# First pass of a feed-forward stage: two result tiles of a block opened side by side, in PSUM banks of their own behind the attention

## The chip, the cores and the metric

One core of a Trainium2 chip runs the whole program. The metric is device time in microseconds (us), from the start of an execution to its end; the median of several executions counts. The engines are TensorE (PE; its weight loads, PEld, overlap its matmuls), VectorE (DVE), ScalarE (ACT), GpSimd (POOL) and SyncE (SP), which here only issues DMAs.

## The reference

Three stages in a row, all in fp32, on 4 x 576 = 2304 tokens of width 512 (8 heads of 64):

```python
scores = where(causal, -1e9, q @ k.T / 8);  a = softmax(scores)
local = a @ v
mem = (phi(q) @ M_prev) / (phi(q) . z_prev + 1e-6)          # phi = elu + 1
x = sigmoid(beta) * mem + (1 - sigmoid(beta)) * local        # to [2304, 512]

x = relu(x @ w_in) ** 2 @ w_out                              # w_in [512, 2048], w_out [2048, 512]

order = argsort(-(x @ w_gate))                               # [2304, 8], greedy, 288 tokens for each expert
out[mask_e] = relu(x[mask_e] @ w1[e]) @ w2[e]                # 8 experts, w1 [512, 1024], w2 [1024, 512]
```

## The kernel before, in words

Matmuls keep fp32 accuracy by splitting each operand into a high and a low half of a narrower float type (`split`, line 23: ACT copies the high half, DVE or POOL subtracts it to get the low one) and multiplying three times (`mm3`, lines 41 to 45: high x high, high x low, low x high).

**Attention** (`attention`, line 48) goes over 16 pairs of heads, in steps that work on several pairs at once. Between its own matmuls it calls `fill` (line 1065), which lets the feed-forward stage put matmuls of its own into TensorE's order. Its PSUM pool has six of the eight banks.

**The feed-forward stage** (class `Ffn`, line 389) runs over 16 chunks of 128 hidden columns in three passes (`PASSES`, line 369: chunks 0 to 5, 6 to 9, 10 to 15), since the split weights of all chunks don't fit beside the rest. The weights come as 64-bit floats, which `weights` (line 411) loads and `narrow` (line 29) converts, with steps on ACT and DVE, a temporary tile `r`, and a last step on POOL.

*The first pass* (`first`, line 464) takes the tokens in eight blocks of 288. `tokens` (line 430) loads a block's attention result (`xf`), adds its halves on POOL, splits it (`xs`, one buffer), and stores it to `xs_d` for the later passes. `hidden` (line 442) multiplies one chunk: 12 matmuls into a PSUM tile `ph` (pool `ffp3`, two banks), then ACT's relu (`r`, line 450), POOL's square (`gf`, line 452) and the split into `gs` on ACT and DVE (lines 25 and 26). After the six chunks come four result tiles, d = 0 to 3, of 128 result columns each (`output`, line 457): 6 chunks x 3 matmuls = 18 matmuls into a tile of the same two banks, ACT's eviction into `yo` (line 483; two buffers, for even and odd d), and SP's store to `yp_d` (line 484). The call of `tokens` for the next block stands ahead of d = 1, or of a later d when the attention has not yet gone far enough. A block is thus 72 hidden and 72 output matmuls.

About four and a half blocks go through `fill` while the attention runs; the rest follows behind it, in a loop (lines 1092 to 1098) that puts in a piece of the conversion of the next pass' weights after every 48 matmuls (temporary tiles `r` in a PSUM pool `cvp` of three banks, raw tiles in `cv`, two buffers).

*The later passes* (`later`, line 486) take the tokens in six steps of 384 per pass. `get` (line 492) loads a step's tokens from `xs_d` into `xt` (line 495; two buffers, 1.5 MB each): the load for step n + 1 is traced after the first hidden tile of step n. Each step loads the sums so far (`y`, line 505), adds its four result tiles to them on DVE (line 522), and stores them again.

**The third stage** (class `Moe`) finds the tokens of each expert (routing) and runs the experts; it starts with the gate's logits, which are taken from the last pass' sums.

**What sets the order of the work.** TensorE's order is that of the program text up to the end of the first pass (`manual_schedule`, line 1081); behind it, and on all other engines and on SP, a scheduler fixes each engine's order when the program is built. On the chip every engine goes through its order and stands at each instruction until what it needs is there. Memory of closed pools is used again; a new tile there waits for the last use of those tiles that lay in the same place (`reuse_waits="tile"`). Before, the two `xt` buffers lie in memory that the attention left; the pool `ga` of `gs` tiles for the later passes and the pool of `y` tiles lie in memory that the first pass leaves.

Of the kernel before, what the change touches and what calls it, by code (L numbers as in the profile page):

```python
# [7 lines left out]
F32 = mybir.dt.float32  # L8
F32R = mybir.dt.float32r
I32 = mybir.dt.int32  # L10
BF16 = mybir.dt.bfloat16
AF = mybir.ActivationFunctionType
OP = mybir.AluOpType
PSUM = bass.MemoryType.PSUM
# [8 lines left out]
def split(nc, hi, lo, src, eng=None):  # L23

    nc.scalar.activation(hi, src, AF.Copy)  # L25
    (eng or nc.vector).tensor_tensor(lo, src, hi.bitcast(F32), op=OP.subtract)  # L26
# [14 lines left out]
def mm3(nc, out, lhi, llo, rhi, rlo, start, stop):  # L41

    nc.tensor.matmul(out, lhi, rhi, start=start, stop=False)  # L43
    nc.tensor.matmul(out, lhi, rlo, start=False, stop=False)  # L44
    nc.tensor.matmul(out, llo, rhi, start=False, stop=stop)  # L45
# [316 lines left out]
TB = 288  # L362
NB_T = NT // TB
TW = 384
NB_W = NT // TW
FF = 2048
KD = DM // 128
KF = FF // 128
PASSES = tuple(tuple(range(a, b)) for a, b in ((0, 6), (6, 10), (10, KF)))
GB = 7  # L370
# [9 lines left out]
def run(work):  # L380

    while True:
        try:
            next(work)
        except StopIteration as e:
            return e.value


class Ffn:
# [5 lines left out]
    def __init__(self, tc, ctx, ident, x_d, xs_d, w_in, w_out, w_gate, yp_d, y_d, lg):  # L395
        self.tc, self.nc, self.ident = tc, tc.nc, ident
        self.x_d, self.xs_d, self.w_in, self.w_out, self.yp_d, self.y_d, self.lg = x_d, xs_d, w_in, w_out, yp_d, y_d, lg
        nc = tc.nc
        one = self.one = ctx.enter_context(tc.tile_pool(name="ff1", bufs=1, side="right"))
        self.two = ctx.enter_context(tc.tile_pool(name="ff2", bufs=2, side="right"))  # L400
        self.p3 = ctx.enter_context(tc.tile_pool(name="ffp3", bufs=2, space=PSUM, side="right"))
        self.start = None
        wg = one.tile([128, KD, 8], F32, name="wg")
        nc.sync.dma_start(wg, w_gate.rearrange("(k p) e -> p k e", p=128))
        self.wgs = one.tile([128, KD, 16], F32R, name="wgs")
        split(nc, self.wgs[:, :, 0:8], self.wgs[:, :, 8:16], wg)
        self.two8 = one.tile([16, 8], F32, name="two8")
        nc.vector.tensor_tensor(self.two8, ident[0:16, 0:8], ident[0:16, 8:16], op=OP.add)
        self.win, self.wout, self.Y, self.have = {}, {}, {}, 0
# [44 lines left out]
        split(nc, G[:, 0], G[:, 1], gf)  # L454
        return G

    def output(self, py, G, cs, d):
        nc, ds = self.nc, slice(128 * d, 128 * d + 128)
        for c in cs:
            w = self.wout[c]  # L460
            mm3(nc, py, w[:, 0, ds], w[:, 1, ds], G[c][:, 0], G[c][:, 1], c == cs[0], c == cs[-1])
            yield 3

    def first(self, gpool):

        nc, xs, cs = self.nc, {}, PASSES[0]
        for i in range(NB_T):
            while self.have <= i:
                yield 0
            if i not in xs:  # L470
                xs[i] = self.tokens(i)
                for _ in range(LAG):
                    yield 0
            G = {}
            for c in cs:
                G[c] = yield from self.hidden(xs[i], c, gpool)
            for d in range(KD):
                if d >= 1 and i + 1 < NB_T and i + 1 not in xs and self.have > i + 1:
                    xs[i + 1] = self.tokens(i + 1)
                py = self.p3.tile([128, TW], F32, name="ph")[:, 0:TB]  # L480
                yield from self.output(py, G, cs, d)
                yo = self.start.tile([128, TB], F32, name=f"yo{d % 2}")
                nc.scalar.activation(yo, py, AF.Copy)
                nc.sync.dma_start(self.yp_d[128 * d:128 * d + 128, TB * i:TB * i + TB], yo)

    def later(self, gpool, beside):


        nc, steps = self.nc, [(p, i) for p in range(1, len(PASSES)) for i in range(NB_W)]
        xs, G, after = {}, {}, []  # L490

        def get(n):
            if n < len(steps):
                t_ = xs[n] = self.xp.tile([128, 2, KD, TW], F32R, name="xt")
                nc.sync.dma_start(t_.bitcast(F32), self.xs_d[:, :, :, TW * steps[n][1]:TW * steps[n][1] + TW])
                G[n] = {}

        def hide(n, c):
            G[n][c] = run(self.hidden(xs[n], c, gpool))

        get(0)
        for n, (p, i) in enumerate(steps):
            cs, final = PASSES[p], p == len(PASSES) - 1
            y = self.Y[i] = self.ty.tile([128, KD, TW], F32, name="y")
            nc.sync.dma_start(y, self.yp_d[:, TW * i:TW * i + TW].rearrange("(k p) t -> p k t", p=128))
            for c in cs:
                if c not in G[n]:
                    hide(n, c)
                if c == cs[0]:
                    get(n + 1)  # L510
                if c == cs[1]:
                    for w in after:
                        w()
                    after = []
                if c % 2 == 0:
                    next(beside, None)
            if n + 1 < len(steps):
                hide(n + 1, PASSES[steps[n + 1][0]][0])
            for d in range(KD):
                py = self.p2x.tile([128, TW], F32, name="py")  # L520
                run(self.output(py, G[n], cs, d))
                nc.vector.tensor_tensor(y[:, d], py, y[:, d], op=OP.add)  # L522
            if not final:
                nc.sync.dma_start(self.yp_d[:, TW * i:TW * i + TW].rearrange("(k p) t -> p k t", p=128), self.Y.pop(i))
            else:
                after = [lambda i=i: self.logits(i)]
                if i < NB_W - HELD:
                    after.append(lambda i=i: run(self.rows(i)))
            del G[n], xs[n]
        for w in after:  # L530
            w()
# [504 lines left out]
def tile_attention_ffn_moe(ctx, tc, q, k, v, M_prev, z_prev, beta, w_in, w_out, w_gate, w1, w2, out):  # L1036
    nc = tc.nc
# [13 lines left out]
    fctx = ExitStack()  # L1051
    f = Ffn(tc, fctx, ident, x_d, xs_d, w_in, w_out, w_gate, yp_d, y_d, lg)
    wa = fctx.enter_context(tc.tile_pool(name="wa", bufs=6, side="right"))

    def chunks(cs, home, pool, psum=None):
        for c in cs:
            for part in range(2):
                yield from f.weights(c, part, home, pool, nc.gpsimd, psum)
# [22 lines left out]
    with tc.manual_schedule(engines=INORDER):  # L1081
        attention(tc, ident, q, k, v, M_prev, z_prev, beta, x_d, fill, ended)
        m.open(ctx, lg)
        f.have = NB_T
        wb = fctx.enter_context(tc.tile_pool(name="wb", bufs=4, reuse_waits="tile"))
        cv = fctx.enter_context(tc.tile_pool(name="cv", bufs=2, reuse_waits="tile"))
        f.t2 = fctx.enter_context(tc.tile_pool(name="ff22", bufs=2, reuse_waits="tile"))
        f.xp = fctx.enter_context(tc.tile_pool(name="ffx", bufs=2, reuse_waits="tile"))
        pctx = ExitStack()
        cp = pctx.enter_context(tc.tile_pool(name="cvp", bufs=3, space=PSUM, side="right", reuse_waits="tile"))  # L1090
        conv, done = chunks(PASSES[1], wb, cv, cp), 0
        for e in work:
            done += e
            if done >= PIECE:
                done -= PIECE
                next(conv, None)
        for _ in conv:
            pass
        pctx.close()
    sctx.close()  # L1100
    f.p2x = fctx.enter_context(tc.tile_pool(name="ffp2x", bufs=2, space=PSUM, side="right", reuse_waits="tile"))
    ga = fctx.enter_context(tc.tile_pool(name="ga", bufs=GB, side="right", reuse_waits="tile"))
    f.ty = fctx.enter_context(tc.tile_pool(name="ffy", bufs=HELD + 1, side="right", reuse_waits="tile"))
    f.later(ga, chunks(PASSES[2], wa, cv))
    held = (x for i in range(NB_W - HELD, NB_W) for x in f.rows(i))

# [37 lines left out]
```

## Time and profile before

| | us |
|---|---|
| median of 3 runs | 1079.33 (1076.73 to 1083.37) |
| the profiled execution | 1079.72 |
| its span, from the first to the last instruction | 1077.60 |

The profile is one execution. Times in it are us from the span's start unless marked ns. A row of the timeline names start, duration, engine, line, operation, the tile written and the tiles read, with shapes (partitions x elements); a bracket behind it gives the idle time of the engine just before it and what ended that. Matmuls are pipelined: the next one starts before the last one's end, and the marked idle time counts from that end.

### The profile page before, as it was taken

The numbers are of one execution on the slowest core, as the hardware profiler recorded it, in microseconds if no ns is written. First come the engines' busy times: TensorE is split into PE (matmuls) and PEld (weight loads), VectorE is DVE, ScalarE is ACT, GpSimd is POOL, SyncE is SP. The second block draws the span as 40 slices with busy tenths as digits, with TensorE's granted clock in tenths as the row PEclk, the third lists the DMA queues.
The fourth block names the chain that finished last, engine by engine and source line by source line (L and its number), as shares of the span: only waits on it lengthen the run. The fifth ranks groups of instructions, "written<-read, shape, count | busy, mean of one in ns | idle before, by whom it ended". The sixth has DMA issues, their size and how long they took to land.

```text
span 1077.6 us, 19670 instructions
## 1 busy us (share of the span) xinstructions
PE 966.5 (90%) x7025; PEld 890.5 (83%) x7025; DVE 641.1 (59%) x1876; ACT 553.0 (51%) x1363; POOL 520.2 (48%) x498
## 2 busy tenths in 40 slices
PE   4766799999999988999999999997399999989996
PEld 3555588887898987999999999995298888889996
DVE  7998888788888846565222222235775677655110
ACT  6776888887888744453222333321243443344531
POOL 3665665656556535354122121110565865677841
PEclk9667899999999999999999999996589999999998
DMA  5453465364635287676463332101542455437411
GB/s 147 120 145 104 110 155 156 85 181 93 173 77 145 61 293 243 189 241 240 171 216 117 117 117 74 75 1 59 179 157 68 156 179 179 135 111 235 152 30 30
DMA packets 147393, 148.62 MB, mean 138 GB/s; under 512 B 69472, under 2 KB 119648, under 8 KB 147296
## 3 DMA queue, kind: packets, MB, share of 16 engines
q1 hardware_dynamic: 144224, 137.93, 41.6%
q0 software_dynamic: 3072, 9.44, 2.8%
q8 instruction: 55, 0.90, 0.3%
q14 instruction: 42, 0.34, 0.1%
HBM read 109.60 MB, written 37.75 MB: 137 GB/s over the span
## 4 chain that ended last, share of the span: by engine, by line
PE 56%; DVE 18%; issue 8%; DMA 7%; ACT 6%; POOL 3%; SPq 1%; another core or an unknown queue 0%; POOLq 0%; ACTq 0%; DVEq 0%
PE ph L945 11%; PE ph L43 6%; PE ph L44 6%; PE ph L45 6%; PE py L44 4%; PE py L43 4%; PE py L45 4%; PE ps L311 3%; DMA wraw<-in_moe_w_dram 3%; PE ps L216 2%; POOL wsp L928 2%; PE rs L727 2%; DVE P L227 2%; DVE ptb L26 2%; DVE qpt L199 2%
## 5 line engine op out<-in xcount | busy, mean ns | idle before, releaser
L452 POOL TENSOR_TENSOR gf<-r 128x384 f32<-128x384 f32 (+1 forms) x108 | 87.3, 810 | 228.8 <-ACT r L450 222.5
L928 POOL TENSOR_TENSOR wsp<-wraw,wsp 128x1024 fp32r<-128x1024 f32 x64 | 150.8, 2386 | 47.2 <-ACT wsp L926 47.0
L945 PE MATMUL ph<-xs,wsp 128*128 128x288 f32 x768 | 122.0, 309 | 0.0
L26 DVE TENSOR_TENSOR gs<-gf,gs 128x384 fp32r<-128x384 f32 (+1 forms) x108 | 60.7, 564 | 97.9 <-ACT gs L25 97.7
L945 PE MATMUL ph<-hs,wsp 128*128 128x288 f32 x768 | 115.9, 304 | 0.7 <-ACT hs L968 0.6
L945 PEld LDWEIGHTS ph<-xs,wsp 128*128 128x128 f32 x768 | 108.4, 195 | 5.3 <-issue 4.2
L245 POOL TENSOR_SCALAR P<-P,R,og 128x128 f32<-128x128 f32 (+2 forms) x144 | 95.4, 677 | 33.5 <-DVE R L243 13.6
L945 PEld LDWEIGHTS ph<-hs,wsp 128*128 128x128 f32 x768 | 105.4, 191 | 2.6 <-issue 0.9
L926 ACT ACTIVATE wsp<-wraw 128x1024 fp32r<-128x1024 f32 x64 | 64.2, 1051 | 57.3 <-DMA wraw<-in_moe_w_dram 38.9
L450 ACT ACTIVATE r<-ph 128x384 f32<-128x384 f32 (+1 forms) x108 | 48.3, 450 | 83.5 <-PE ph L45 82.0
L239 ACT ACTIVATE P<-P,R 128x128 f32<-128x128 f32 (+2 forms) x144 | 83.2, 579 | 10.9 <-DVE R L227 9.2
L25 ACT ACTIVATE gs<-gf 128x384 fp32r<-128x384 f32 (+1 forms) x108 | 52.6, 487 | 62.7 <-POOL gf L452 50.7
L44 PE MATMUL py<-gs,wout 128*128 128x384 f32 x240 | 81.0, 338 | 0.1
L44 PE MATMUL ph<-xt,win 128*128 128x384 f32 x240 | 80.8, 337 | 0.0
L45 PE MATMUL ph<-xt,win 128*128 128x384 f32 x240 | 80.8, 337 | 0.0
L43 PE MATMUL ph<-xt,win 128*128 128x384 f32 x240 | 80.7, 336 | 0.0
L45 PE MATMUL py<-gs,wout 128*128 128x384 f32 x240 | 80.5, 336 | 0.0
L43 PE MATMUL py<-gs,wout 128*128 128x384 f32 x240 | 79.2, 338 | 0.3 <-DVE y L522 0.3
L270 PE MATMUL ps<-ident,P 128*128 128x128 f32 x320 | 62.7, 305 | 12.5 <-POOL P L245 4.8
L216 PE MATMUL ps<-kt,qt 64*128 64x128 f32 (+3 forms) x384 | 59.4, 390 | 14.7 <-DVE ptb L26 7.0
L43 PE MATMUL ph<-xs,win 128*128 128x288 f32 x192 | 62.2, 324 | 4.0 <-ACT r L450 1.9
L26 DVE TENSOR_TENSOR ptb<-ps,ptb 128x384 fp32r<-128x384 f32 (+3 forms) x128 | 59.5, 467 | 8.9 <-ACT ptb L25 7.2
(227 smaller groups left out, 2537.2 us busy)
## 6 DMA issues: line engine op xcount, KB each, us to landing
wraw<-in_moe_w_dram SPq DMA_DIRECT2D x32, 1024.0 KB, 9.6
xt<-xs_d SPq DMA_DIRECT2D x12, 1536.0 KB, 7.7
x_d<-xo SPq DMA_DIRECT2D x32, 288.0 KB, 3.5
xf<-x_d SPq DMA_DIRECT2D x32, 288.0 KB, 3.5
xs_d<-xs SPq DMA_DIRECT2D x8, 1152.0 KB, 6.7
y<-yp_d SPq DMA_DIRECT2D x12, 768.0 KB, 6.4
raw<-in_moe_w_in_dram SPq DMA_DIRECT2D x16, 512.0 KB, 3.8
raw<-in_moe_w_out_dram SPq DMA_DIRECT2D x16, 512.0 KB, 3.6
```

The lines of the kernel that those rows point to most:

```text
L26: (eng or nc.vector).tensor_tensor(lo, src, hi.bitcast(F32), op=OP.subtract)
L43: nc.tensor.matmul(out, lhi, rhi, start=start, stop=False)
L44: nc.tensor.matmul(out, lhi, rlo, start=False, stop=False)
L45: nc.tensor.matmul(out, llo, rhi, start=False, stop=stop)
L216: nc.tensor.matmul(ps[j][:, 0:w], qt[r0, a, qs], kt[r0, b, 0:w], start=i == 0, stop=i == 2)
L239: nc.scalar.activation(pw, pw, AF.Exp, bias=R[:, 0, u:u + 1], scale=-1.0, accum_out=R[:, 1, u:u + 1])
L245: nc.gpsimd.tensor_scalar(PP[n][w], PP[n][w], R[:, 2, w:w + 1], og9[:, hp, w:w + 1], op0=OP.mult, op1=OP.mult)
L270: nc.tensor.transpose(tr[:, 128 * i:128 * i + 128], P[:, 128 * i:128 * i + 128], ident)
L452: nc.gpsimd.tensor_tensor(gf, r, r, op=OP.mult)
L926: nc.scalar.activation(w[:, 0, hs], raw[:, hs], AF.Copy)
L928: eng.tensor_tensor(w[:, 1, hs], raw[:, hs], w[:, 0, hs].bitcast(F32), op=OP.subtract)
L945: nc.tensor.matmul(out, l[a], r[b], start=i + p == 0, stop=i == n - 1 and p == 2)
```

## The change

In `first`, the result tiles are taken in three groups: d = 0 and 1 together, then 2, then 3. The tiles of a group are opened together; each takes the first four chunks in turn, then each takes the last two and is evicted. `tokens` for the next block is called ahead of d = 2 or 3. As long as the attention runs, the result tiles come from the two `ph` banks as before; behind it they come from a pool `ffpo` with two banks of its own, and `cvp` has two banks instead of three.

The two `xt` buffers become two pools of one buffer: the first in memory that the attention left, the second in memory that the first pass leaves. `ga` changes to memory that the attention left; the pool `ff22` (tiles of `logits` and `rows`) changes to memory that the first pass leaves.

```diff
--- before.py
+++ after.py
@@ -399,7 +399,7 @@
         one = self.one = ctx.enter_context(tc.tile_pool(name="ff1", bufs=1, side="right"))
         self.two = ctx.enter_context(tc.tile_pool(name="ff2", bufs=2, side="right"))
         self.p3 = ctx.enter_context(tc.tile_pool(name="ffp3", bufs=2, space=PSUM, side="right"))
-        self.start = None
+        self.start, self.pout, self.po = None, self.p3, "ph"
         wg = one.tile([128, KD, 8], F32, name="wg")
         nc.sync.dma_start(wg, w_gate.rearrange("(k p) e -> p k e", p=128))
         self.wgs = one.tile([128, KD, 16], F32R, name="wgs")
@@ -454,9 +454,9 @@
         split(nc, G[:, 0], G[:, 1], gf)
         return G
 
-    def output(self, py, G, cs, d):
+    def output(self, py, G, cs, d, part=slice(None)):
         nc, ds = self.nc, slice(128 * d, 128 * d + 128)
-        for c in cs:
+        for c in cs[part]:
             w = self.wout[c]
             mm3(nc, py, w[:, 0, ds], w[:, 1, ds], G[c][:, 0], G[c][:, 1], c == cs[0], c == cs[-1])
             yield 3
@@ -474,14 +474,17 @@
             G = {}
             for c in cs:
                 G[c] = yield from self.hidden(xs[i], c, gpool)
-            for d in range(KD):
-                if d >= 1 and i + 1 < NB_T and i + 1 not in xs and self.have > i + 1:
+            for ds in ((0, 1), (2,), (3,)):
+                if ds[0] and i + 1 < NB_T and i + 1 not in xs and self.have > i + 1:
                     xs[i + 1] = self.tokens(i + 1)
-                py = self.p3.tile([128, TW], F32, name="ph")[:, 0:TB]
-                yield from self.output(py, G, cs, d)
-                yo = self.start.tile([128, TB], F32, name=f"yo{d % 2}")
-                nc.scalar.activation(yo, py, AF.Copy)
-                nc.sync.dma_start(self.yp_d[128 * d:128 * d + 128, TB * i:TB * i + TB], yo)
+                py = {d: self.pout.tile([128, TW], F32, name=self.po)[:, 0:TB] for d in ds}
+                for part in (slice(0, 4), slice(4, None)):
+                    for d in ds:
+                        yield from self.output(py[d], G, cs, d, part)
+                        if part.stop is None:
+                            yo = self.start.tile([128, TB], F32, name=f"yo{d % 2}")
+                            nc.scalar.activation(yo, py[d], AF.Copy)
+                            nc.sync.dma_start(self.yp_d[128 * d:128 * d + 128, TB * i:TB * i + TB], yo)
 
     def later(self, gpool, beside):
 
@@ -491,7 +494,7 @@
 
         def get(n):
             if n < len(steps):
-                t_ = xs[n] = self.xp.tile([128, 2, KD, TW], F32R, name="xt")
+                t_ = xs[n] = self.xp[n % 2].tile([128, 2, KD, TW], F32R, name="xt")
                 nc.sync.dma_start(t_.bitcast(F32), self.xs_d[:, :, :, TW * steps[n][1]:TW * steps[n][1] + TW])
                 G[n] = {}
 
@@ -1084,10 +1087,12 @@
         f.have = NB_T
         wb = fctx.enter_context(tc.tile_pool(name="wb", bufs=4, reuse_waits="tile"))
         cv = fctx.enter_context(tc.tile_pool(name="cv", bufs=2, reuse_waits="tile"))
-        f.t2 = fctx.enter_context(tc.tile_pool(name="ff22", bufs=2, reuse_waits="tile"))
-        f.xp = fctx.enter_context(tc.tile_pool(name="ffx", bufs=2, reuse_waits="tile"))
+        x0 = fctx.enter_context(tc.tile_pool(name="ffx0", bufs=1, reuse_waits="tile"))
+        ga = fctx.enter_context(tc.tile_pool(name="ga", bufs=GB, reuse_waits="tile"))
         pctx = ExitStack()
-        cp = pctx.enter_context(tc.tile_pool(name="cvp", bufs=3, space=PSUM, side="right", reuse_waits="tile"))
+        cp = pctx.enter_context(tc.tile_pool(name="cvp", bufs=2, space=PSUM, side="right", reuse_waits="tile"))
+        f.pout = pctx.enter_context(tc.tile_pool(name="ffpo", bufs=2, space=PSUM, side="right", reuse_waits="tile"))
+        f.po = "po"
         conv, done = chunks(PASSES[1], wb, cv, cp), 0
         for e in work:
             done += e
@@ -1099,8 +1104,10 @@
         pctx.close()
     sctx.close()
     f.p2x = fctx.enter_context(tc.tile_pool(name="ffp2x", bufs=2, space=PSUM, side="right", reuse_waits="tile"))
-    ga = fctx.enter_context(tc.tile_pool(name="ga", bufs=GB, side="right", reuse_waits="tile"))
     f.ty = fctx.enter_context(tc.tile_pool(name="ffy", bufs=HELD + 1, side="right", reuse_waits="tile"))
+    x1 = fctx.enter_context(tc.tile_pool(name="ffx1", bufs=1, side="right", reuse_waits="tile"))
+    f.t2 = fctx.enter_context(tc.tile_pool(name="ff22", bufs=2, side="right", reuse_waits="tile"))
+    f.xp = x0, x1
     f.later(ga, chunks(PASSES[2], wa, cv))
     held = (x for i in range(NB_W - HELD, NB_W) for x in f.rows(i))
```

## Rows read from the trace of the kernel before

**Rows 1.** The page, section 1: busy us, share of the span, instructions.
```profile
PE 966.5 (90%) x7025; PEld 890.5 (83%) x7025; DVE 641.1 (59%) x1876; ACT 553.0 (51%) x1363; POOL 520.2 (48%) x498
```

**Rows 2.** Stretches: length, busy PE, PEld, DVE, ACT, POOL; PE clock, DMA, GB/s.
```profile
383.00:462.00 79.00, 69.77 (x475) 66.00 (x475) 40.24 (x62) 37.04 (x85) 34.26 (x37) 0.96 0.74 239
462.00:718.00 256.00, 255.88 (x1486) 250.05 (x1485) 87.61 (x158) 85.80 (x169) 62.89 (x69) 1.00 0.42 143
```

**Rows 3.** The same view, shorter stretches behind the attention.
```profile
392.10:400.60 8.50, 8.35 (x60) 8.12 (x61) 5.39 (x9) 5.13 (x14) 4.51 (x6) 1.00 0.97 325
...
424.50:431.00 6.50, 3.58 (x20) 2.66 (x19) 6.50 (x11) 2.96 (x7) 3.85 (x5) 0.89 0.49 156
431.00:436.30 5.30, 5.30 (x24) 5.30 (x24) 3.87 (x7) 3.31 (x7) 3.61 (x4) 0.50 0.74 220
```

**Rows 4.** TensorE's waits from 383 to 462: us in total, times, longest.
```profile
PE ph L44 <- DVE gs L26: 3.7, 6, 1.4
PE ph L43 <- ACT r L450: 1.9, 2, 1.7
PE ph L43 <- ACT yo L483: 1.8, 1, 1.8
PE ph L43 <- ACT gs L25: 1.4, 3, 0.5
```

**Rows 5.** TensorE's timeline: starts of result tiles, and chunk 5's low half in one.
```profile
400.62 0.29 PE L43 MATMUL ph<-gs,wout 128*128 128x288 f32 x1
...
424.54 0.30 PE L43 MATMUL ph<-gs,wout 128*128 128x288 f32 x1
...
430.56 0.61 PE L44 MATMUL ph<-gs,wout 128*128 128x288 f32 x1 [0.89 <-DVE gs L26]
430.96 0.44 PE L45 MATMUL ph<-gs,wout 128*128 128x288 f32 x1
431.20 0.44 PE L43 MATMUL ph<-gs,wout 128*128 128x288 f32 x1
...
450.63 0.30 PE L43 MATMUL ph<-gs,wout 128*128 128x288 f32 x1
...
457.36 0.30 PE L43 MATMUL ph<-gs,wout 128*128 128x288 f32 x1
...
459.75 0.29 PE L43 MATMUL ph<-gs,wout 128*128 128x288 f32 x1
```

**Rows 6.** DVE's timeline: last low halves of the three blocks, and of tokens.
```profile
403.70 0.81 DVE L26 TENSOR_TENSOR gs<-gf,gs 128x288 fp32r<-128x288 f32 x2
...
412.74 0.95 DVE L26 TENSOR_TENSOR xs<-xf,xs 128x288 fp32r<-128x288 f32 x1
...
430.06 0.45 DVE L26 TENSOR_TENSOR gs<-gf,gs 128x288 fp32r<-128x288 f32 x1
...
454.08 0.44 DVE L26 TENSOR_TENSOR gs<-gf,gs 128x288 fp32r<-128x288 f32 x1
```

**Rows 7.** Timeline of ACT and of TensorE: the first hidden tiles behind the attention.
```profile
391.69 0.41 ACT L483 ACTIVATE yo<-ph 128x288 f32<-128x288 f32 x1 [4.87 <-DMA yp_d<-yo]
...
392.16 0.40 PE L43 MATMUL ph<-xs,win 128*128 128x288 f32 x1 [1.85 <-ACT yo L483]
```

**Rows 8.** All evictions by tile (ns min/median/max), stores, and the eviction that started latest.
```profile
L483 ACT ACTIVATE yo<-ph x32: 387/404/414, 174.8 to 462.4; 128x288 f32<-128x288 f32 x32
...
DMA to landing us min/median/max: 1.7/2.9/6.0
...
224.93 0.29 PE L45 MATMUL ph<-gs,wout 128*128 128x288 f32 x1
...
228.92 0.39 ACT L483 ACTIVATE yo<-ph 128x288 f32<-128x288 f32 x1
```

**Rows 9.** The two token loads on SP's queue, and the landing of all twelve.
```profile
392.55 1.47 SPq L495 DMA_DIRECT2D xt<-xs_d  x2
...
DMA to landing us min/median/max: 6.9/7.7/10.0
```

## The prediction

> **What bounds the kernel now.** I read the busy shares of the page first: TensorE is busy for 90% of the span and no other engine for more than 59% [rows 1]. An average over stages with different limits says little of one stage, so the next view is the table of stretches. There the reader sees the stage that the change aims at, the end of the first pass behind the attention: 69.77 us of 79.00 busy, while the later passes behind it are full, 255.88 of 256.00 [rows 2]. A result tile's 18 matmuls take 459.75 - 457.36 = 2.39 us, so one matmul follows the last by 0.133 us [rows 5]. This stage issues 475 of them, which is 63.2 us of work in 79.0: 15.8 us are lost. That is all that the change can win here, 1.5% of the run; and as the later passes leave TensorE no idle time and the routing starts from their result, what is won arrives at the end whole.
>
> Where the 15.8 us lie is in the table of waits of TensorE in this stretch [rows 4]: output matmuls waiting for the low and high half of `gs` (3.7 and 1.4 us of marked idle time), and hidden matmuls waiting for an eviction `yo` (1.8). The marks leave out what lies in an overlap, so I count from starts. The shape is the same in all three blocks left behind the attention. When the last hidden tile of a block has been multiplied, its relu, its square, its high half and its low half follow one another on ACT, POOL, ACT and DVE, while the first result tile (d = 0) wants chunk 5's low half as its 17th matmul, 16 x 0.133 = 2.1 us after it starts. It starts at 400.62, 424.54 and 450.63 [rows 5]; that half is ready at 404.51, 430.51 and 454.52 [rows 6], so 3.9, 6.0 and 3.9 us later. TensorE loses 1.8, 3.9 and 1.8 us. In the second block there is more: the granted clock is 1.00 before and 0.50 (1.2 instead of 2.4 GHz) from 431.0 to 436.3, where 24 matmuls are counted; at 0.24 instead of 0.133 us that is some 22 x 0.107 = 2.4 us [rows 3, 5].
>
> **The change part by part.** *Two result tiles side by side.* d = 0 and d = 1 each take four chunks first, then d = 0 the last two, then d = 1. No matmul is added. Chunk 5's low half is now wanted as the 29th matmul instead of the 17th, 12 x 0.133 = 1.6 us later. Against delays of 1.8, 3.9 and 1.8 us this recovers 1.6 us in each of three blocks, 4.8 in all; the bounds are nothing (the halves come later by as much) and 4.8. In the five blocks inside the attention nothing is to be had: the table of waits of the whole run gives the low halves the same 3.7 us as this stretch alone [rows 4], so none of it lies there, where attention matmuls stand between.
>
> *The clock.* In the second block 2.3 of the 3.9 us stay. The fall came after 3.58 busy us of 6.50 [rows 3]; other gaps of about 2 us (before 392.16, and the 1.8 us of the first block) left the clock at 1.00. I take it that it does not fall: 2.4 us won, bounds 0 and 2.4. The Trainium skill, "TensorE: Matmul & The Clock Gate", section "What's actually happening", puts it the other way round: the throttled state is the default, and activity releases it. The trace agrees as far as the fall after the emptiest stretch goes [rows 3], but by that rule a stretch that still holds 2.3 us of gaps has no claim to the full clock, and the gain would be 2.4 us less, 1075.7.
>
> *Banks of their own.* Behind the attention result tiles leave the two banks of `ph`. Before, the hidden matmul at 392.16 waited for the eviction at 391.69, itself held for 4.87 us by the store of an earlier `yo` [rows 7]; 2.0 us were lost. Now two hidden tiles (24 matmuls, from 388.55 to 391.75) run past that, and the third waits for the relu of the first, which stands behind the same eviction on ACT: 391.69 + 0.41 + 0.4 = 392.45, a wait of 0.7. Won: 1.3, bounds 0 and 2.0. The conversion loses one of three PSUM buffers; it has two raw buffers only, so I cost that at nothing; if the third did count, the conversion for the later passes would be late, which nothing before 462 reads.
>
> *What is late next: the third result tile.* It takes the bank of d = 0. Before, that tile was 18 matmuls old when d = 2 began; now d = 0 ends six matmuls before, so 7 x 0.133 = 0.93 us lie between the start of its last matmul and d = 2. In that time the matmul has to end (0.29), ACT has to get to the eviction, and the eviction takes 0.40 [rows 8]. Over the 32 evictions the start on ACT comes between 0.04 us and 3.70 us after the last matmul's end (224.93 + 0.29 = 225.22, to 228.92, rows 8, the longest); the mean is 0.70 for the last twelve and 1.14 for the sixteen of the first four blocks. So behind the attention 0.29 + 0.70 + 0.40 - 0.93 = 0.46 us of wait in each of three blocks, 1.4. Inside the attention other matmuls lie between: from the 30th output matmul's start to the 37th's the first four blocks have 0.9, 4.2, 1.6 and 2.4 us, where 0.29 + 1.14 + 0.40 = 1.83 is wanted, so waits of 0.9, 0, 0.2 and 0. Cost: 2.5 us; bounds 0 and 3.5 in each of seven blocks. Queued behind a waiting matmul is all of TensorE's order, the attention's too. A second wait falls on ACT: the `yo` buffer of d = 2 is that of d = 0, stored 3.2 us before; that store lands after 1.7 to 6.0 us [rows 8], and ACT may stand for 3 us with relus behind it, but TensorE has d = 3 and two hidden tiles (5.6 us) in front.
>
> *Tokens.* Their call moves from d = 1 to d = 2. Loads and adds are put where the engines are free, so I cost this at nothing; but the last low half of the second block's tokens was done at 413.69 [rows 6], with that block's first hidden matmul at 412.33, so if the tokens come no sooner than now, the first block's 1.6 us are lost again: bounds 0 and 1.6.
>
> *The second token buffer.* Now one buffer is filled at 392 instead of two [rows 9]; 1.5 MB leave a stretch where the DMA engines are busy 0.97 at 325 GB/s [rows 3], 4.8 us of their time, which speaks for earlier weights and tokens (nothing counted). Its memory is that of the first pass, so its load can start only when the last `gs` has been read, at 462; it lands 6.9 to 10.0 us later [rows 9]. Step 0 has 48 hidden matmuls for that (48 x 256.00 / 1486 = 8.3 us, rows 2), and 8.3 us of outputs that can go first. Nothing counted; bounds 0 and 9 (below).
>
> The sum: 4.8 + 2.4 + 1.3 - 2.5 = 6.0 us off the profiled execution's 1079.72 (span 1077.60 and 2.12 around it) gives 1073.7; the median of the three runs is 0.39 lower, so 1073.3.
>
> **The rivals.** A, *the bank of the third tile decides.* One mechanism: d = 2's first matmul waits for ACT to evict d = 0, in every block. For it speaks that ACT's order is fixed and that an eviction has stood 3.70 us behind other work [rows 8]; against it that the last twelve stood 0.70 us on the mean. It turns the sign where the mean wait over eight blocks passes 8.5 / 8 = 1.06 us; at 1.5 us it costs 12.0 against 8.5, so 1079.3 + 3.5 = 1082.8. The Trainium skill, "Perfetto Trace Analysis", section "Optimization Strategy", reads the same gap coming back over a stretch as too little PSUM for the next tile; by that rule this gap is to be looked for in front of d = 2 in all blocks. The trace of before has no such gap there, so no row decides.
>
> B, *the second buffer comes too late.* If its load shares the engines with three `y` loads (2.3 MB, 7 us at the 325 GB/s of rows 3), it lands up to 17.6 us after 462; TensorE has 8.3 us without it, or 16.6 with the outputs first. Between 0 and 9.3 us, at the middle 1073.3 + 4.6 = 1077.9.
>
> C, *the relief counts.* With the weights' loads landing sooner, the waits for relus queued behind a conversion (1.9 us marked, rows 4, and 2.2 from starts) go, and the 0.7 left in front of the third hidden tile; the third result tile waits nowhere: 8.5 + 2.2 + 0.7 = 11.4, so 1079.3 - 11.4 = 1067.9.
>
> D, *the halves come later too.* DVE is busy for 6.50 of 6.50 us in the second block's wait [rows 3]; if DVE sets the pace there, its 1.6 and the clock's 2.4 stay lost, and the sum is 6.0 - 4.0: 1077.3.
>
> **How the numbers follow.** My forecast has 0.50, with 1070 to 1077 as its own range; A 0.10, B 0.11, C 0.15, D 0.14. The wanted range takes in C nearly and A in part: 1067.5 to 1082. A measurement of this kernel can tell about 1% from no change, and the stage holds 1.5%: faster by more (under 1068.5) is most of C and a tail of the forecast, 0.14; slower by more (over 1090) needs A at 2.4 us a block, or A with B, 0.05; the rest, 0.81.
>
> **What would show it.** Right: in the three blocks behind the attention no wait for `gs` over 0.3 us in the first and third and about 2 in the second; the clock at 1.00 there; the hidden matmul after the attention waiting for a relu, not for `yo`; one token load near 392 and one right after the first pass; the first pass ending near 456. Wrong: TensorE waiting for `yo` in front of d = 2 by over 1 us a block; a wait for the second token tile in the first later step; or an attention stage that ends at another time than 383.

## The result and the profile after

The changed kernel takes 1086.64 us (median of 20 runs, 1080.98 to 1095.31) beside 1079.88 for the kernel before on the same chip; the ratio is 1.0069, 95% interval 1.0046 to 1.0092. It is slower by 0.7%, where the prediction had it faster by 0.6%. The profiled execution has a span of 1083.7 us against 1077.6.

Busy time hardly moved, TensorE's by 2.4 us; the page of after answers to [rows 1]:

```profile
PE 968.9 (89%) x7025; PEld 892.9 (82%) x7025; DVE 642.8 (59%) x1876; ACT 552.8 (51%) x1363; POOL 521.8 (48%) x498
```

So 6 us of idle time or of slow clock were added. The stretches of after, with the columns of [rows 2], say where:

```profile
383.00:462.00 79.00, 71.04 (x500) 69.53 (x499) 43.21 (x65) 38.65 (x90) 35.88 (x40) 0.98 0.69 217
462.00:718.00 256.00, 248.51 (x1422) 241.44 (x1421) 88.95 (x153) 80.32 (x160) 60.04 (x64) 0.99 0.44 150
...
392.90:396.00 3.10, 3.08 (x18) 3.08 (x19) 0.34 (x1) 1.27 (x4) 0.67 (x1) 0.75 0.81 254
396.00:400.00 4.00, 4.00 (x26) 4.00 (x26) 3.81 (x7) 2.02 (x6) 1.54 (x2) 0.76 0.95 344
...
430.00:437.00 7.00, 6.22 (x47) 6.17 (x47) 5.40 (x8) 3.38 (x8) 3.37 (x4) 1.00 0.87 261
462.00:474.70 12.70, 7.43 (x43) 6.78 (x41) 7.11 (x9) 2.92 (x6) 6.57 (x5) 0.93 0.74 252
474.70:479.70 5.00, 4.99 (x16) 4.99 (x17) 0.98 (x2) 0.00 (x0) 0.00 (x0) 0.50 1.07 373
```

The first stretch holds 500 matmuls instead of 475: TensorE got more done by 462, and its clock stayed up at 430 to 437, where it had fallen before [rows 3]. But the first pass itself ends no sooner: its last matmul starts at 462.58, before at 461.99. The text ahead of the prediction says that TensorE's order is that of the program text up to the end of the first pass; for the changed kernel that doesn't hold. From 448.01 on, 36 hidden matmuls of the first later step (step 0; steps are counted from 0) stand among the last block's output matmuls:

```profile
448.01 0.34 PE L43 MATMUL ph<-xt,win 128*128 128x384 f32 x1
```

The stretch behind it, which had no idle time, lost 7.4 busy us and 64 matmuls [rows 2], most of them between 462 and 480.

TensorE's waits of after, from 383 to 462 and from 462 to 718, name two different stories:

```profile
PE ph L43 <- ACT yo L486: 3.4, 1, 3.4
PE ph L43 <- ACT r L450: 2.3, 2, 2.1
PE po L44 <- DVE gs L26: 2.2, 3, 1.0
...
PE py L43 <- DVE y L525: 6.0, 3, 4.0
PE py L44 <- DVE gs L26: 1.5, 2, 1.3
```

In the first pass the waits for `gs` went from 3.7 and 1.4 us [rows 4] to 2.2. Behind it there is a new wait, for the add into `y`, the sums that the first pass stored and the first later step loads again. In the timeline of TensorE:

```profile
392.92 0.40 PE L43 MATMUL ph<-xs,win 128*128 128x288 f32 x1 [3.44 <-ACT yo L486]
407.59 0.40 PE L44 MATMUL po<-gs,wout 128*128 128x288 f32 x1 [1.03 <-DVE gs L26]
429.38 0.40 PE L44 MATMUL po<-gs,wout 128*128 128x288 f32 x1 [0.42 <-DVE gs L26]
430.83 0.40 PE L44 MATMUL po<-gs,wout 128*128 128x288 f32 x1 [0.78 <-DVE gs L26]
469.73 0.44 PE L44 MATMUL py<-gs,wout 128*128 128x384 f32 x1 [1.28 <-DVE gs L26]
474.71 0.69 PE L43 MATMUL py<-gs,wout 128*128 128x384 f32 x1 [4.00 <-DVE y L525]
475.20 0.52 PE L44 MATMUL py<-gs,wout 128*128 128x384 f32 x1
475.52 0.52 PE L45 MATMUL py<-gs,wout 128*128 128x384 f32 x1
...
479.68 0.40 PE L43 MATMUL py<-gs,wout 128*128 128x384 f32 x1
```

At 474.71 TensorE has stood 4.00 us for a bank that DVE had yet to read; then the matmuls follow one another by 0.32 us instead of 0.17 until 479.68, at the granted clock of 0.50 of the stretch above. 1.28 + 4.00 + 16 x (0.32 - 0.17) = 7.7 us lost in ten. Why DVE was late is in its own timeline, which shows a gap of 4.42 us and names no releaser ("issue"):

```profile
474.10 1.02 DVE L525 TENSOR_TENSOR y<-py,y 128x384 f32<-128x384 f32 x2 [4.42 <-issue]
```

The add reads `py`, long done, and `y`. The trace also keeps the times at which each load's completions came, which the views above don't print: those of this `y`, issued at 465.63, came from 473.63 to 474.02, and the add starts at 474.10. So DVE waited for the load of `y`. SP's queue of after:

```profile
465.01 0.57 SPq L498 DMA_DIRECT2D xt<-xs_d  x1
465.63 0.65 SPq L508 DMA_DIRECT2D y<-yp_d  x1
466.34 0.57 SPq L498 DMA_DIRECT2D xt<-xs_d  x1
467.14 5.21 SPq L508 DMA_DIRECT2D y<-yp_d  x2
```

and that of before, which loads the three `y` first and a token tile nine us later:

```profile
463.22 1.54 SPq L505 DMA_DIRECT2D y<-yp_d  x3
...
472.09 0.57 SPq L495 DMA_DIRECT2D xt<-xs_d  x1
```

Which token tile is which these rows don't say; the order written for SP in the program does. In its lines for the changed kernel the tiles have numbers that grow with the steps (`y_6467` and `xt_6489` are made in step 0, for steps 0 and 1; `xt_6652` is made in step 1, for step 2):

```
xt_6652<-xs_d    (tokens of the third step, into the first buffer)
y_6467<-yp_d     (sums of the first step)
xt_6489<-xs_d    (tokens of the second step, into the second buffer)
y_6650<-yp_d, y_6813<-yp_d
```

SP's waits from 440 to 480 agree: one token load waited for a hidden matmul, so it goes into the buffer that step 0's hidden matmuls read (the last of them starts at 464.64, the load at 465.01).

```profile
SPq L498 <- PE ph L45: 1.2, 1, 1.2
```

So the tokens of the *third* step, 1.5 MB that TensorE first reads at 491, went ahead of the sums that the first step needed at 470.7, when its first result tile was done. Those tokens' last completion came at 471.91, the sums' 2.1 us behind it.

To follow gains and losses along the run I counted how much feed-forward work TensorE had done by a point of time (each matmul at its spacing, 0.133 us at 288 columns, 0.1735 at 384), minus the kernel before, in us. Each column is one profiled execution:

```
   at   after   e1    e2    e3    e4    e5    e6    e7    e8
  384    0.8   1.5   2.4   2.3   2.3   1.1   0.7   3.9   0.3
  420   -2.1   1.3   0.8   2.7   2.8   0.7   1.2   2.3  -2.9
  438    4.0   6.7   4.3   7.8   8.1   5.3   2.9   8.5   3.2
  456    5.7   7.6   4.3   8.6  10.3   5.1   4.9   8.8   3.8
  468    5.7   7.6   3.6   6.6  10.4   4.7   4.9   6.6   3.8
  480   -2.1   8.0   3.8   4.9  10.8   5.0   5.0   0.5   1.9
  516   -5.4   6.8   3.3   4.3   9.4   4.9   4.9  -1.6   0.7
```

After is 5.7 us ahead at 468, 2.1 behind at 480, and 5.4 behind at 516, and stays about there: its last output matmul of the later passes starts at 737.38 instead of 731.74. Columns differ by up to 3.6 us at 384 already, ahead of the stage, and a column is one execution: those of e2 and e4 are the shortest of twelve runs, that of e5 the longest. So read a column by how it moves down, and the worth of a kernel from its median.

### The profile page after: what moved, and what is told of

Its sections match the earlier page's. It is cut to its first block, busy times and chain, and to the rows that moved or that the text cites. A ratio compares the mean times of both kernels' runs of the same rounds, so it can differ in the third digit from the quotient of the medians.

```text
span 1083.7 us, 19660 instructions
## 1 busy us (share of the span) xinstructions
PE 968.9 (89%) x7025; PEld 892.9 (82%) x7025; DVE 642.8 (59%) x1876; ACT 552.8 (51%) x1363; POOL 521.8 (48%) x498
## 4 chain that ended last, share of the span: by engine, by line
PE 56%; DVE 18%; issue 7%; ACT 7%; DMA 7%; POOL 3%; SPq 1%; another core or an unknown queue 0%; POOLq 0%; ACTq 0%; DVEq 0%
PE ph L948 11%; PE ph L43 6%; PE ph L44 6%; PE ph L45 6%; PE py L43 4%; PE py L44 4%; PE py L45 4%; PE ps L311 3%; DMA wraw<-in_moe_w_dram 3%; PE ps L216 2%; POOL wsp L931 2%; PE rs L730 2%; DVE qpt L199 2%; ACT P L239 2%; PE ps L270 2%
## 5 line engine op out<-in xcount | busy, mean ns | idle before, releaser
L26 DVE TENSOR_TENSOR gs<-gf,gs 128x384 fp32r<-128x384 f32 (+1 forms) x108 | 66.0, 613 | 94.4 <-ACT gs L25 94.3
L43 PE MATMUL py<-gs,wout 128*128 128x384 f32 x240 | 80.9, 345 | 6.3 <-DVE y L525 6.3
L44 PE MATMUL py<-gs,wout 128*128 128x384 f32 x240 | 82.1, 342 | 1.5 <-DVE gs L26 1.5
L45 PE MATMUL py<-gs,wout 128*128 128x384 f32 x240 | 81.5, 340 | 0.0
L525 DVE TENSOR_TENSOR y<-py,y 128x384 f32<-128x384 f32 x48 | 26.1, 556 | 67.7 <-PE py L45 63.3
```

## The experiments

My theory after the result (M): the second buffer and the `y` tiles lie in the first pass' memory, so their loads are squeezed together behind it, and `y` comes late. The rival (O): the new order itself, or what the scheduler makes of it, costs the time.

**e1: order and banks, SBUF places of before.**

```diff
-        x0 = ... tile_pool(name="ffx0", bufs=1 ...); ga = ... tile_pool(name="ga", bufs=GB ...)
+        f.t2 = ... tile_pool(name="ff22", bufs=2 ...); f.xp = ... tile_pool(name="ffx", bufs=2 ...)
...
-    x1 = ... tile_pool(name="ffx1", bufs=1, side="right" ...); f.t2 = ...; f.xp = x0, x1
+    ga = ... tile_pool(name="ga", bufs=GB, side="right" ...)
```

> The result tiles side by side and their own PSUM banks, with the SBUF places of the kernel before (both token buffers and the tiles of logits in memory left by the attention, gs tiles in memory left by the first pass). Theory M (the time is lost behind the first pass, because the second token buffer and the sums y can be loaded only when the first pass has ended): what the first pass wins stays, so about 5 us less than before, ratio 0.995. Rival O (the order itself costs, by waits that it adds on TensorE and ACT): about as slow as the changed kernel, ratio 1.006.

Measured: 0.9946 (0.9922 to 0.997), 1075.17 us. O falls: order and banks gain 0.5%. Stretches; of TensorE's waits from 462 to 520 the only one left is 0.7 us for `gs`:

```profile
383.00:462.00 79.00, 72.20 (x509) 69.61 (x508) 42.35 (x64) 37.96 (x88) 38.46 (x40) 1.00 0.73 238
462.00:520.00 58.00, 57.33 (x328) 57.00 (x328) 36.51 (x52) 23.09 (x44) 26.01 (x23) 1.00 0.79 269
```

**e2: SBUF places alone**, the kernel before with the pools of after (the reverse of e1's edit).

> Only the SBUF places of the change (second token buffer and the tiles of logits in memory left by the first pass, gs tiles in memory left by the attention); order and banks of the kernel before. Theory M: the loss of 8 to 11 us between 462 and 516 comes without the gain, ratio 1.007 to 1.010, with TensorE waiting for the adds to y near 470. Rival O: no difference, ratio 1.000.

Measured: 1.0025 (0.9999 to 1.0052), 1083.65 us. Theory M in this form asked for more, and TensorE has no marked wait from 462 to 520. Late memory is not enough. SP's order fits that: here the scheduler put the first `y`, the second step's tokens, the other `y` and the next weights ahead of the third step's tokens (at 467.92).

```profile
458.98 0.43 SPq L505 DMA_DIRECT2D y<-yp_d  x1
459.50 0.57 SPq L495 DMA_DIRECT2D xt<-xs_d  x1
460.48 1.82 SPq L505 DMA_DIRECT2D y<-yp_d  x2
...
467.92 0.57 SPq L495 DMA_DIRECT2D xt<-xs_d  x1
```

**e3: first sums early.** After, with the first `y` tile in memory that the attention left.

```diff
+        y0 = ... tile_pool(name="ffy0", bufs=1, reuse_waits="tile")
-        ga = ... tile_pool(name="ga", bufs=GB ...)
+        ga = ... tile_pool(name="ga", bufs=6 ...)
...
+    y1 = ... tile_pool(name="ffy", bufs=HELD, side="right" ...); f.ty = Turns(y0, y1, y1)
+    gb = ... tile_pool(name="gb", bufs=GB - 6, side="right" ...)
```

(`Turns` hands out tiles of its pools in turn.)

> The changed kernel, with the first y tile in memory left by the attention (one of seven gs tiles goes to the first pass' memory for it), so that its load need not wait for the first pass. Theory M with y as what comes last: the wait of 4.0 us for DVE's add and the slow clock behind it (2.3 us) go, about 1080, ratio 1.000 or below. Theory M with the second token buffer as what comes last: TensorE waits for the tokens of step 1 instead, ratio 1.004 to 1.007. Rival O: ratio 1.006.

Measured: 1.0008 (0.9978 to 1.0039), 1081.63 us. The wait for `y` is nearly gone; a smaller one for the second step's tokens, which here too stand behind the third step's, took its place (TensorE's waits, 462 to 520):

```profile
PE ph L43 <- DMA xt<-xs_d: 1.7, 1, 1.7
...
PE py L43 <- DVE y L535: 0.3, 1, 0.3
```

**e4: both token buffers early.** After, with both `xt` in the attention's memory, and four `gs` tiles there and the rest in the first pass'.

```diff
-        x0 = ... tile_pool(name="ffx0", bufs=1 ...); ga = ... tile_pool(name="ga", bufs=GB ...)
+        x0 = ... tile_pool(name="ffx0", bufs=2 ...); ga = ... tile_pool(name="ga", bufs=4 ...)
...
-    x1 = ...; f.xp = x0, x1
+    f.xp = x0, x0; gb = ... tile_pool(name="gb", bufs=GB - 4, side="right" ...)
```

> The changed kernel, with both token buffers in memory left by the attention (three of seven gs tiles go to the first pass' memory for it). Theory M: step 1 can start without a load, the outputs of step 0 come later and y has time to land: 5 us less than before, ratio 0.995. Theory M with y alone: y is as late as in the changed kernel, ratio 1.003 to 1.006. Rival O: ratio 1.006.

Measured: 0.9957 (0.993 to 0.9984), 1077.06 us; the stretch behind the first pass is full again:

```profile
462.00:520.00 58.00, 57.24 (x328) 56.60 (x327) 35.68 (x50) 21.55 (x42) 25.63 (x22) 1.00 0.79 273
```

**e5 and e6: the two halves of e1 apart.** e5 is the kernel before with the new order alone (tiles from `ph`); e6 has the banks of their own alone.

```diff
# e5, against e1
-        cp = ... tile_pool(name="cvp", bufs=2 ...); f.pout = ... tile_pool(name="ffpo", bufs=2 ...); f.po = "po"
+        cp = ... tile_pool(name="cvp", bufs=3 ...)
# e6, against e1
-            for ds in ((0, 1), (2,), (3,)): ...
+            for d in range(KD): ...
```

> The kernel before with the new order of the result tiles and nothing else: d = 0 and d = 1 side by side from the two banks of the hidden tiles, three PSUM buffers for the conversion, SBUF places as before. With the banks of their own added, the same gave 0.9946 of before. If the order alone brings that (the low halves wanted 1.6 us later in each of three blocks, and the clock that stays up): ratio 0.994 to 0.997. If the side by side order needs the banks (d = 0 and d = 1 hold both banks, and the next tiles stand behind their evictions): 0.999 to 1.003.

> The kernel before with result tiles in two banks of their own behind the attention (the conversion has two PSUM buffers) and nothing else: d = 0 to 3 one after the other, SBUF places as before. The prediction gave the banks 1.3 us, bounds 0 and 2.0: ratio 0.998 to 1.000. If the wait for the eviction behind the attention stays, because the last tiles of the fifth block still lie in the banks of the hidden tiles: 1.000 to 1.002, with that wait at 392 still in the trace.

Measured: e5 0.9954 (0.9928 to 0.9979), 1076.54 us; e6 0.9985 (0.9951 to 1.0018), 1079.57 us. The order alone brings what e1 has, within the intervals; of the banks nothing can be told from no change. Stretches of e5, then of e6, and in e6's timeline the matmul of [rows 7], which waits as before:

```profile
424.00:430.00 6.00, 4.17 (x27) 3.36 (x25) 4.96 (x10) 3.38 (x10) 2.23 (x3) 1.00 0.53 151
430.00:437.00 7.00, 6.80 (x49) 6.56 (x50) 4.62 (x8) 3.93 (x10) 3.17 (x4) 1.00 0.74 251
```

```profile
430.00:437.00 7.00, 7.00 (x44) 7.00 (x44) 4.41 (x8) 3.23 (x7) 2.53 (x2) 0.78 0.86 273
...
391.46 0.40 PE L43 MATMUL ph<-xs,win 128*128 128x288 f32 x1 [1.76 <-ACT yo L483]
```

In e6, with the order of before, the clock falls in that stretch (0.78); in e5, with the new order, it does not (1.00). That is no proof that the order decides it: e2 has the order of before too, its clock is 1.00 from 430 to 437, and its second block loses 2.2 us (its result tiles start from 422.53 to 434.22, where 71 x 0.133 = 9.4 would do), against 6.5 before and 6.2 in e6.

e6 also shows what the banks do. As in every kernel here with banks of their own (after, e1, e3, e4, e6, e7, e8) and in none without (before, e2, e5), hidden matmuls of step 0 stand among the last block's outputs.

**e7: second buffer asked for later.** After, with `get(1)` behind the first result tile of step 0 in the program text, and no hidden tile of step 1 asked for ahead of step 0's outputs.

```diff
-                if c == cs[0]:
+                if c == cs[0] and n:
                     get(n + 1)
...
-            if n + 1 < len(steps):
+            if 0 < n and n + 1 < len(steps):
...
+                if n == 0 and d == 0:
+                    get(1)
```

> The changed kernel, with the load of the second token buffer asked for behind the first result tile of the first later step instead of ahead of it, and no hidden tile of the second step ahead of that step's outputs. If the sums y are late because they share queue and DMA engines with the second buffer's load: y lands by 470, the wait of 4.0 us for it at 474.7 goes, the second buffer is wanted at about 480 and lands near then, so the ratio to before falls from 1.007 to 1.000 to 1.004. If the memory of y itself comes free too late: y still starts at 465 or later, the wait stays at 2 to 4 us, and the late second buffer adds to it: 1.007 to 1.015.

Measured: 1.007 (1.0033 to 1.0107), 1088.21 us. As a test of its question it is void: the scheduler wrote the same order for SP, as the queue's timeline shows (token tile, `y`, token tile, two `y`), only 3 us earlier:

```profile
461.96 0.57 SPq L498 DMA_DIRECT2D xt<-xs_d  x1
462.58 0.65 SPq L508 DMA_DIRECT2D y<-yp_d  x1
463.29 0.57 SPq L498 DMA_DIRECT2D xt<-xs_d  x1
464.09 5.35 SPq L508 DMA_DIRECT2D y<-yp_d  x2
...
471.77 0.69 PE L43 MATMUL py<-gs,wout 128*128 128x384 f32 x1 [4.22 <-DVE y L525]
```

It shows two things all the same: `y`'s first add still has to wait until 471.16, and where a load stands in the text does not decide where it stands in the queue. SP's written order led to the last theory (Q): not the late memory as such, but the third step's tokens at the head of the queue.

**e8: third step's tokens behind the first sum.** After, plus one VectorE instruction that writes one column of the token tile from `y`, so that its load has to wait for that (`first` is a list of the `y` tiles; the lines that fill it are cut).

```diff
                 t_ = xs[n] = self.xp[n % 2].tile([128, 2, KD, TW], F32R, name="xt")
+                if n == 2:
+                    nc.vector.tensor_scalar(t_[:, 0, 0, 0:1], first[0][:, 0, 0:1], 0.0, None, op0=OP.add)
```

> The changed kernel with one tiny VectorE instruction (128 x 1, from the first sum y into the token tile of the third step) that holds that tile's load back until the first sum is made. In the changed kernel SP's order behind the first pass is: tokens of the third step, y of the first, tokens of the second, y of the second and third. Theory Q (the queue): the 1.5 MB of the third step's tokens, not wanted until after 495, stand ahead of the first y and of the second step's tokens, and y, issued at 465.63, has its adds only at 474.10. With them behind, y is issued near 464 and lands by 470; the wait of 4.0 us at 474.7 and the clock's fall behind it go: ratio to before 0.998 to 1.003. Theory M alone (y and the second buffer both start only when the first pass's memory is free, whatever stands ahead of them): y's adds start at 472 or later, a wait of 2 to 4 us for y or for the second tokens stays: 1.004 to 1.009.

Measured: 0.997 (0.9944 to 0.9996), 1079.29 us, against 1.0069 for the same kernel without that one instruction. SP's queue of e8, then the landing of the first `y` (KB, us), then DVE's and TensorE's timelines:

```profile
465.74 0.39 SPq L511 DMA_DIRECT2D y<-yp_d  x1
466.18 0.57 SPq L500 DMA_DIRECT2D xt<-xs_d  x1
467.20 2.06 SPq L511 DMA_DIRECT2D y<-yp_d  x2
...
473.46 0.57 SPq L500 DMA_DIRECT2D xt<-xs_d  x1
...
y<-yp_d SPq DMA_DIRECT2D x1, 768.0 KB, 5.0
...
472.30 1.02 DVE L528 TENSOR_TENSOR y<-py,y 128x384 f32<-128x384 f32 x2 [0.71 <-PE py L45]
473.24 0.14 DVE L499 TENSOR_SCALAR xt<-y 128x1 fp32r<-128x1 f32 x1
...
471.65 0.44 PE L44 MATMUL py<-gs,wout 128*128 128x384 f32 x1 [1.26 <-DVE gs L26]
472.92 0.45 PE L43 MATMUL py<-gs,wout 128*128 128x384 f32 x1 [0.30 <-DVE y L528]
```

`y` lands 5.0 us after its issue, though 1.5 MB of tokens follow it 0.44 us later. In after the same load, issued as early (465.63), had 1,536 KB ahead of it, which at the 373 GB/s of its stretch 474.7 to 479.7 take 4.2 us, and which were issued 0.62 us sooner: 5.0 + 4.2 - 0.6 = 8.6, and it landed 8.4 us after the issue, at 474.02. DVE now waits for the matmul and not for the load, TensorE waits 0.30 instead of 4.00 us, and the clock does not fall (1.00 from 462 to 520). The Trainium skill, "DMA: Bandwidth & Descriptors", section "Queues, rings and completion order", says that each DMA engine takes the descriptors of one queue in the order of its ring; these two landings agree with that, and no run here shows single descriptors.

The scheduler wrote a somewhat different order for TensorE in e8 too, so not every tenth of a us is the queue's. But three kernels that each take away a different part of the jam (the sums from it in e3, the second buffer in e4, the third step's tokens in e8) bring back 0.6, 1.1 and 1.0%.

## Why the prediction was wrong

*The stage it aimed at won about what was forecast, in part by other ways.* The sum was 6.0 us; after is 0.8 us ahead at 384 and 5.7 at 456, so 4.9 were won. The first pass did not end near 456, as the signs of being right had it, but at 462.58: 36 x 0.1735 = 6.2 us of step 0's hidden matmuls stand in front of that. The terms:

- Side by side, 4.8 us: right for two blocks of three. Counted from starts, the result tiles of the three blocks lost 1.9, 6.5 (2.4 of it the clock) and 1.9 us before, and 1.4, 1.8 and nothing in after. The first block kept more than the 0.3 of my sign, the second less than the 2.3 left for it. The third block's gain is not the new order's: e5, which has that order without the banks, still loses 2.1 there, and in after step 0's hidden matmuls fill the wait. By itself (e5) the order is worth 1 - 0.9954 = 0.46%, 5 us.
- The clock at 431 to 436: it came as forecast, the reason is open. It stays at 1.00 in after, e1 and e5, and falls in e6, which has the old order; but it stays at 1.00 in e2 too, which has the old order. The rule that I weighed there (the Trainium skill, "TensorE: Matmul & The Clock Gate", section "What's actually happening": the throttled state is the default, and activity releases it), as I used it, spoke for a fall; the 1.00 of 430 to 437 decides for after, where the second block has 1.2 us of marked waits for the low half and not the 2.3 that I reckoned with. (I read 1.00 ahead of 431.0, where rows 3 have 0.89 from 424.5 to 431.0: it fell at about 429.6, inside the wait.)
- Banks of their own, +1.3: not won. The hidden matmul behind the attention waited 3.44 us for the same eviction, after 1.85 [rows 7], and its clock then fell: 44 matmuls from 392.9 to 400, where 7.1 / 0.133 = 53 fit, another 1.2. The longer wait goes with the order and not with the banks: it is 2.80 us in e5 (the order alone) and 1.76 in e6 (the banks alone). What the banks did bring, the third block above, stands in no term. The premise failed. I took all result tiles behind the attention to lie in the new banks. But that block's last tiles were put into TensorE's order by the attention's last calls, before the new banks exist, so d = 2 and d = 3 still held both banks of `ph`. (A slip besides: 391.69 + 0.41 + 0.4 is 392.50, not 392.45.) The timeline of ACT shows the second `yo<-ph` there:

```profile
392.46 0.41 ACT L486 ACTIVATE yo<-ph 128x288 f32<-128x288 f32 x1 [6.46 <-DMA yp_d<-yo]
```

- The third result tile, -2.5: too dear. No matmul of after waits in front of d = 2 behind the attention; e1, e3 and e4 have one such wait each, of 0.4 to 0.6 us. That is also the end of rival A: the gap to look for by the Trainium skill, "Perfetto Trace Analysis", section "Optimization Strategy", is not there.
- Tokens at nothing: no matmul of after waits for the first pass' tokens; e1 has one such wait behind the attention, of 0.4 us.

*The step that failed* is "The second token buffer. ... Nothing counted; bounds 0 and 9". I asked whether TensorE would run out of tokens for step 1, found 8.3 us of hidden matmuls and 8.3 of "outputs that can go first", and called it covered. The scheduler did put the outputs first, and outputs need `y`. Before, the first `y` was wanted at 478.9 and issued at 463.22; in after it was wanted at 470.7, and two token loads joined it in the queue, one of them ahead. I costed the moved load by its own reader and not by what it stands beside on SP's queue. The term measured 5.7 + 5.4 = 11.1 us between 468 and 516: 7.8 by 480 and 3.3 after it (of these 0.2, 0.4 and 1.7 are marked waits, the longest again for `y`'s add). 5.7 - 11.1 = -5.4, and the medians moved by 6.8.

Rival B was the nearest. It had the place, and the sharing with the `y` loads, but a different victim (the second token tile, which TensorE never waited for in after), 4.6 us as its middle (its upper end should be 10.0 + 7.3 = 17.3 us and not 17.6), and a chance of 0.11. Its sign of failure, "a wait for the second token tile in the first later step", would not have caught what happened; it shows in e3 alone. C and D did not decide: the relu waits stayed (2.3 us), and the clock's gain came.

What stays open: why the scheduler puts the third step's tokens at the head in after and not in e2 was not tried. The rows offer part of a reason: that load can go when step 0's last hidden matmul has read its buffer, and with banks of their own those matmuls run ahead of the last outputs (464.64 in after, 467.55 in e2; the load follows 0.37 us later in both); but e1 and e4 have the banks too, and there two `y` go first. e8 still loses 3.1 us between 456 and 516 where e1 loses 0.8, which may be the price of the second buffer's place, but the intervals of e1 and e8 overlap. The fastest version measured is e1, 0.9946, with e5 and e4 beside it: the change without its move of the second buffer beats both kernels.

## What to carry to other kernels

When a load is moved, write down the queue's whole order behind the point that it moves to, with the bytes ahead of each load and the time at which each is wanted; the load that suffers is often another one. "The other work can go first" is only true when everything that the other work reads is there by then. And where the order is a scheduler's, moving a line of the text may move nothing (e7), while one tiny data dependence that holds back the load least wanted can bring 1% (e8).

## What the runs showed of the hardware that I had not expected

The granted clock fell behind single waits at the head of busy work, but not by their length alone. Behind the attention it was 0.75 from 392.9 to 396 after a wait of 3.44 us (after), 0.56 from 392.1 to 396 after 2.80 us (e5) and 0.63 from 391.4 to 396 after 1.76 us (e6); it stayed at 1.00 after 1.85 us (before, [rows 3, 7]) and from 390 to 400 after 2.24 us (e1). What tells these apart no run here shows. After waits of 1.28 and 4.00 us it was 0.50 from 474.7 to 479.7, which added 2.4 us to 5.3 us of waiting.

And a gap that ends with "issue" can be a wait for a transfer: the 4.42 us of DVE at 474.10 have no releaser in the view, and ended 0.08 us after the load's last completion.
